# Windowed attention with soft experts: keys in blocks of 64 on stacked partitions, one exp per unit, TensorE in program order

## Chip, cores and metric

The kernel runs on one core of a Trainium2 chip. The metric is the device time of one execution in microseconds (us), the median of several runs. A profile is one execution taken by the hardware profiler; its span runs from the first to the last instruction of the program.

## The reference

Eight batches, eight heads, 576 positions of 64 numbers. Heads 0 to 3 attend to the last 32 positions, heads 4 to 7 to every fourth of the last 128. The result goes, as 4608 rows of 512, into a soft mixture of 8 experts with 4 slots each.

```python
scores = scale * np.matmul(q, k.transpose(0, 1, 3, 2))
rel = pos[:, None] - pos[None, :]
mask_plain = (rel >= 0) & (rel < 32)
mask_dil = (rel >= 0) & (rel < 32 * 4) & (rel % 4 == 0)
attn = softmax(where(mask, scores, -1e9));  x = attn @ v      # rows of 512
logits = x @ phi                                               # 4608 x 32
slot_input = softmax(logits over the rows).T @ x               # 32 x 512
slot_out[e] = relu(slot_input[e] @ w1[e]) @ w2[e]              # e of 8 experts
return softmax(logits over the slots) @ slot_out
```

Every input and the output are fp32 in HBM: q, k and v of 9.4 MB each, 33.6 MB of weights, 9.4 MB of output.

## The kernel before

**Loads.** GpSimd's queue (POOL) issues all large loads in program order (`load_batch`, L184 and L162): for each batch q, k and v, cast to fp16, into one of eight tiles `home`. The weights follow into the same tiles: `load_w1(e)` (L239) and `load_w2(e)` (L250) reuse the home of batch e once its readers are through, and stand in the main loop at the third of a batch's four units.

**Units.** A batch has four units `u` of two heads, in the order plain, dilated, plain, dilated (`unit`). A plain unit works on the 32-wide window in blocks of 128 keys (`NKB` = 5, the last one half full), each met by `QW` = 160 queries. A dilated unit sorts positions by their remainder by 4: four classes of 144, one block of 128 keys each and 16 left over, whose keys are gathered in a fifth block.

For each unit:

- `transposes(u)` (L275, L290): q and k are transposed on TensorE into the PSUM pool `ring` (2 buffers) and copied out (L280, L295) into `qT` (2 buffers) and `kTp` or `kTd`.
- `scores(u)` (L315): keys by queries into two PSUM tiles of pool `ps_s` (2 buffers of two banks). The two heads lie on the two halves of the partitions.
- `softmax_parts(u)`: exp on ScalarE, two per unit (L332 plain, L344 dilated); products with the 0/1 mask on VectorE (L335 plain, three; L353 and L360 dilated).
- `values(u)` (L395): probabilities by v (with a column of ones, which gives the sum) into two PSUM tiles of pool `ps_o` (2 buffers), all 128 keys per matmul; then reciprocal (L399) and product (L400) on VectorE, once per half.
- `x_transposes(u)` (L416): x is transposed into `ring` and copied to `xT` (L420, L422, L426).

`select_v(b)` (L205, L216, L225) rearranges a batch's v on TensorE with the 0/1 matrix `pick`, 32 rows a time, and copies it to `vp` on ScalarE; `spread_v` (L194) does the dilated heads' part on VectorE. `front_logits`, `front_rows` and `front_slots` turn a finished batch into logits, their exp `ET`, and the running sum over slots, a few units later.

**End.** After the last unit `last_early`, `last_logits` and `last_slots` finish the slots; `expert_in` (L675, L683, L686, L691) and `expert_out` (L699) run the eight experts in pairs; the sum `sop` is copied to `so` (L716); 38 matmuls `f` (L735) with copies on ScalarE and VectorE (L739, L741) make the output, which SyncE's queue stores (L745, L747).

**Order.** Only POOL keeps the order of the program (`manual_schedule`). The other engines' order is made by the scheduler of the framework from its own estimates.

## Time and profile before

| | us |
|---|---|
| median of 3 runs (185.67 to 186.18) | 185.69 |
| span of the profiled execution | 183.5 |
| TensorE matmul busy, 2595 instructions | 151.8 |
| VectorE busy, 363 | 117.1 |
| ScalarE busy, 208 | 115.5 |
| POOL busy, 77 | 46.9 |

41.06 MB, the output among them, pass the DMA queues; HBM is read for 62.02 MB and written for 9.44 MB. Some groups of instructions, with their count, the busy time of all and the mean of one:

| line, engine | what | count | us | mean ns |
|---|---|---|---|---|
| L332 ScalarE | exp, 128x960 | 16 | 15.8 | 989 |
| L332 ScalarE | exp, 128x448 | 16 | 9.1 | 572 |
| L344 ScalarE | exp, 128x640 | 32 | 20.9 | 706 |
| L335 VectorE | mask product, 128x960 | 16 | 10.3 | 646 |
| L353 VectorE | mask product, 128x1024 | 16 | 10.8 | 676 |
| L399 VectorE | reciprocal, 128x6 and 128x4 | 64 | 10.2 | 177 |
| L400 VectorE | normalising, 128x384 | 32 | 17.5 | 547 |
| L400 VectorE | normalising, 128x256 | 32 | 13.3 | 416 |
| L395 TensorE | values, 128 rows | 288 | 12.9 | 203 |
| L315 TensorE | scores, 64 rows, 160 wide | 128 | 11.1 | 256 |
| L735 TensorE | f, 512 wide | 34 | 10.6 | 417 |

Busy times of an engine's groups overlap where instructions are pipelined, so a matmul's duration is not what it costs in a row of matmuls; the distance from start to start is. In lines of the profile PE is TensorE, PEld its weight loads, DVE VectorE, ACT ScalarE, SP SyncE; a "q" behind an engine is its sequencer; behind an arrow stands what ended the idle time. PEclk in the slices is the clock that TensorE was granted, in tenths of full speed.

### The profile page before, as it was taken

What the parts mean: (1) busy time and instruction counts of PE and PEld (TensorE: products, weight loads), DVE (VectorE), ACT (ScalarE), POOL (GpSimd) and SP (SyncE); (2) the same over time, 40 slices, a digit from 0 to 9 for tenths busy, and PEclk for the clock granted to TensorE, in tenths of its full rate; (3) what the DMA queues carried; (4) which work ended last, traced back from release to release, by engine and by line L of the source; (5) the groups of instructions that cost most, each with busy time, mean ns of one, the idle gap of its engine ahead of it and who ended that gap; (6) DMA issues with size and microseconds to landing.
All of it is one profiled execution on the core that took longest, in us unless ns stands there. A gap on an engine that the chain in (4) does not pass through costs nothing.

```text
span 183.5 us, 6054 instructions
## 1 busy us (share of the span) xinstructions
PE 151.8 (83%) x2595; PEld 105.8 (58%) x2595; DVE 117.1 (64%) x363; ACT 115.5 (63%) x208; POOL 46.9 (26%) x77
## 2 busy tenths in 40 slices
PE   1869999999988989998997998898979998885300
PEld 1637776677676667666765767666768644432000
DVE  7605886388877877878779687786970111496410
ACT  2248845689599789779878959977703022675410
POOL 7752555464554654401102001003100000000000
PEclk9999999999999999999999999999995589998555
DMA  5999999999999999999999999999999995199996
GB/s 103 183 203 203 202 203 201 202 202 204 204 201 201 204 199 204 226 211 221 212 216 216 212 216 216 218 212 218 218 214 220 212 208 105 75 440 427 427 427 262
DMA packets 23978, 41.06 MB, mean 224 GB/s; under 512 B 1680, under 2 KB 20240, under 8 KB 21136
## 3 DMA queue, kind: packets, MB, share of 16 engines
q0 software_dynamic: 21584, 30.79, 93.9%
q1 hardware_dynamic: 2368, 9.89, 13.4%
q8 instruction: 20, 0.33, 0.6%
q14 instruction: 6, 0.05, 0.1%
HBM read 62.02 MB, written 9.44 MB: 389 GB/s over the span
## 4 chain that ended last, share of the span: by engine, by line
DMA 74%; issue 15%; POOL 3%; ACT 2%; DVE 1%; PE 0%; POOLq 0%; DVEq 0%; SPq 0%
DMA home<-in_moe_w_dram 31%; DMA home<-in_v_dram 15%; DMA home<-in_k_dram 12%; DMA home<-in_q_dram 9%; DMA out_dram<-ot 7%; ACT ot L739 2%; DVE ot L741 1%; POOL home L250 1%; POOL home L162 1%; POOL home L239 1%; POOL home L184 0%; POOL home L187 0%; ACT so L716 0%; PE sop L699 0%; PE f L735 0%
## 5 line engine op out<-in xcount | busy, mean ns | idle before, releaser
L400 DVE TENSOR_TENSOR x<-o,rc 128x384 f16<-128x384 f32 x64 | 29.9, 482 | 0.5
L332 ACT ACTIVATE pr<-s 128x960 f16<-128x960 f32 (+1 forms) x32 | 24.7, 780 | 1.8 <-PE s L315 1.8
L344 ACT ACTIVATE pd<-s 128x640 f16<-128x640 f32 x32 | 20.9, 706 | 1.7 <-PE s L315 1.7
L162 POOL DMA_DIRECT2D home<-in_v_dram x24 | 16.6, 692 | 16.6 <-DMA home<-in_k_dram 11.6
L205 PE MATMUL sel<-home,pick 32*128 32x256 f16 x128 | 17.8, 307 | 1.4 <-DMA home<-in_v_dram 1.1
L399 DVE RECIPROCAL rc<-o 128x6 f32<-128x6 f32 x64 | 10.2, 177 | 13.5 <-PE o L395 13.4
L416 PE MATMUL rgx<-ident,x 128*128 128x128 f16 x160 | 15.6, 233 | 3.0 <-ACT qT L295 3.0
L741 DVE TENSOR_SCALAR ot<-f,rrow 128x512 f32<-128x512 f32 (+1 forms) x19 | 12.5, 716 | 7.7 <-DMA out_dram<-ot 5.2
L335 DVE TENSOR_TENSOR Pp<-pr,mask 128x960 f16<-128x960 f16 (+2 forms) x48 | 16.4, 394 | 0.4 <-ACT pr L332 0.4
L280 ACT COPY qT<-rgq 128x576 f16<-128x576 f16 x16 | 10.3, 641 | 9.0 <-PE rgq L275 8.5
L422 ACT COPY xT<-rgx 128x512 f16<-128x512 f16 x16 | 9.6, 601 | 10.0 <-PE rgx L416 10.0
L739 ACT ACTIVATE ot<-f,rrow 128x512 f32<-128x512 f32 (+1 forms) x19 | 11.2, 675 | 7.0 <-DMA out_dram<-ot 6.6
L239 POOL DMA_DIRECT2D home<-in_moe_w_dram x8 | 4.3, 534 | 44.4 <-PE rgq L290 36.5
L213 ACT CAST vp<-sel 128x512 f16<-128x512 f32 x16 | 9.4, 590 | 9.2 <-PE sel L205 9.0
L416 PEld LDWEIGHTS <-x 128*128 128x128 f16 x160 | 10.2, 102 | 7.2 <-issue 5.4
L735 PE MATMUL f<-so,ET 128*128 128x512 f16 (+1 forms) x38 | 11.0, 402 | 3.9 <-ACT ot L739 3.0
L275 PEld LDWEIGHTS <-home 96*64 96x64 f16 x384 | 11.9, 123 | 3.9 <-issue 2.0
L184 POOL DMA_DIRECT2D home<-in_k_dram x16 | 10.6, 661 | 10.1 <-DMA home<-in_q_dram 8.2
L395 PE MATMUL o<-vp,Pp 128*128 128x65 f16 x288 | 12.9, 203 | 0.0
L436 PE MATMUL l<-xT,phi 128*128 128x288 f16 x64 | 10.8, 304 | 2.0 <-ACT qT L280 1.7
L295 DVE COPY kTd<-rgk 128x576 f16<-128x576 f16 x16 | 12.0, 752 | 0.6 <-PE rgk L290 0.5
L295 ACT COPY qT<-rgq 128x576 f16<-128x576 f16 x16 | 10.3, 646 | 3.1 <-PE rgq L290 2.6
(105 smaller groups left out, 292.9 us busy)
## 6 DMA issues: line engine op xcount, KB each, us to landing
home<-in_moe_w_dram POOLq DMA_DIRECT2D x15, 1024.0 KB, 30.1
out_dram<-ot SPq DMA_DIRECT2D x7, 1024.0 KB, 7.5
home<-in_k_dram POOLq DMA_DIRECT2D x16, 288.0 KB, 9.9
home<-in_q_dram POOLq DMA_DIRECT2D x15, 288.0 KB, 9.7
home<-in_v_dram POOLq DMA_DIRECT2D x16, 256.0 KB, 9.8
out_dram<-ot SPq DMA_DIRECT2D x3, 512.0 KB, 6.5
home<-in_moe_w_dram POOLq DMA_DIRECT2D x2, 512.0 KB, 27.3
home<-in_v_dram POOLq DMA_DIRECT2D x8, 64.0 KB, 8.9
```

Source lines behind the costliest of these rows:

```text
L162: nc.gpsimd.dma_start(out=dst, in_=v[b, h0 : h0 + n_h, r0 : r0 + 4 * n_p, :].rearrange("h (p r) d -> p h (r d)", r=4),)
L205: nc.tensor.matmul(sel[:, n, 0], pick[rows, r].rearrange("p i j -> p (i j)"), raw[rows, :, r, :], start=(r == 0), stop=(r == 3), tile_posi ...
L275: nc.tensor.transpose(rg[64 * h : 64 * h + 64, r, :], raw[:, 2 * hp + h, D * r : D * r + D], ident[0:NP, 0:NP],)
L295: (nc.scalar.copy if nm == "q" else nc.vector.tensor_copy)(out=dst[:, 0:S].rearrange("c (g p a) -> c g p a", g=4, a=3), in_=rg.rearrange(" ...
L332: nc.scalar.activation(out=pr, in_=st[:, :, 0:n], func=AF.Exp, scale=SCALE)
L335: nc.vector.tensor_tensor(out=Pp[:, :, b0 : b0 + nb, 0:w], in0=pr[:, :, at : at + nb * w].rearrange("p h (t c) -> p h t c", c=w), in1=mask ...
L344: nc.scalar.activation(out=pr[:, part].rearrange("p c e t -> p e c t"), in_=st[:, :, 0 : 2 * DW].rearrange("p e (c t) -> p e c t", c=2), f ...
L395: nc.tensor.matmul(to, lhs, rhs, start=(n == 0), stop=(n == len(mms) - 1), skip_group_check=True)
L400: nc.vector.tensor_tensor(out=x[:, blocks[0] : blocks[0] + nb, D * hl : D * hl + 2 * D].rearrange("p t (h d) -> p t h d", h=2), in0=ot[:, ...
L416: nc.tensor.transpose(rg[:, 128 * blk : 128 * blk + 128], x[:, blk, hl : hl + 128], ident)
L739: nc.scalar.activation(out=ot[:, j, d0:d1], in_=fp, func=AF.Copy, scale=scale)
L741: nc.vector.tensor_scalar(out=ot[:, j, d0:d1], in0=fp, scalar1=scale, scalar2=None, op0=ALU.mult)
```

## The change

Keys go in blocks of 64 instead of 128. Two blocks lie on the lower (`LOW`) and upper (`UP`) 64 partitions of one tile and each meets `QW` = 96 queries, so a plain unit's scores are 20 matmuls of 64 rows, 64 keys and 96 queries in a single tile `st`, and there is one exp and one mask product. A dilated unit has 16 such matmuls and 8 of 16 queries for the keys left over, one exp and two products. In `values` each matmul takes the 64 keys of one half; those of head 0's lower half go in turn with those of head 1's upper half, then, after a fence, the other two halves. The fence is an empty instruction on SyncE between the two groups. One reciprocal and one product normalise the whole unit.

`ps_s` and `ps_o` have one buffer of two banks each, `ring` has four of one; `qT` becomes two fixed tiles. `select_v` uses 64 rows a time, and the end of v has its own `select_ends`. TensorE keeps program order as POOL does, and the loop's order is written out anew: scores of the next unit, transposes, the front part of an earlier batch, `select`, first part of `values`, `x_transposes` of the unit before, second part of `values`. The experts' order becomes: input of pair n+1, transposes of pair n, output of pair n. Masks and constants follow the new blocks.

```diff
-QW = 160
+HB = 64
+QW = HB + WINDOW
+SLOT = 192
+TAIL = 16
+SLOT_D = 48 + QW
+LOW, UP = slice(0, HB), slice(HB, 128)
...
-    ring = ctx.enter_context(
-        tc.tile_pool(name="ring", bufs=2, space=bass.MemoryType.PSUM)
-    )
-    ps_o = tc.alloc_tile_pool(name="ps_o", bufs=2, space=bass.MemoryType.PSUM)
-    ps_s = tc.alloc_tile_pool(name="ps_s", bufs=2, space=bass.MemoryType.PSUM)
+    ring = tc.alloc_tile_pool(name="ring", bufs=4, space=bass.MemoryType.PSUM)
+    ps_o = tc.alloc_tile_pool(name="ps_o", bufs=1, space=bass.MemoryType.PSUM)
+    ps_s = tc.alloc_tile_pool(name="ps_s", bufs=1, space=bass.MemoryType.PSUM)
...
     def select_v(b):
+        sel = [ring.tile([128, 2, 4, D], FP32, name=f"sel{b}_{i}", tag="ring") for i in range(2)]
+        for n in range(2):
+            for r in range(4):
+                for i, part in enumerate((LOW, UP)):
+                    nc.tensor.matmul(sel[i][:, n], pick[part, n, r].rearrange("p i j -> p (i j)"), raw[part, :, r, :],
...
     def scores(u):
+        st = ps_s.tile([128, 2, 512], FP32, name=f"s{u}", tag="s")
+        def score(rows, g, at, k0, q0, n):
+            half = slice(HB * g, HB * g + HB)
+            nc.tensor.matmul(
+                st[rows, g, at : at + n],
+                kT[half, k0 : k0 + rows.stop - rows.start],
+                qT[half, q0 : q0 + n],
...
+        if hp < 2:
+            for blk in range(NKB):
+                for g in range(2):
+                    for s, rows in enumerate((LOW, UP)):
+                        k0 = 128 * blk + HB * s
+                        score(rows, g, QW * blk, k0, min(k0, S - HB), QW)
+            return st
+        for i in range(4):
+            for g in range(2):
+                score(LOW, g, QW * i, CL * i, CL * i, QW)
+                score(UP, g, QW * i, CL * i + HB, CL * (i + 1) - QW, QW)
+        for i in range(4):
+            for g in range(2):
+                q0 = CL * i + 128
+                c = 2 * (i // 2) + g
+                score(slice(0, 128), g, 4 * QW + TAIL * i, q0 - HB - TAIL * c, q0, TAIL)
...
     def softmax_parts(u, st):
+        n = NKB * QW if hp < 2 else 4 * (QW + TAIL)
+        nc.scalar.activation(out=pr, in_=st[:, :, 0:n], func=AF.Exp, scale=SCALE)
         if hp < 2:
+            nc.vector.tensor_tensor(
+                out=Pp[:, :, :, HB : HB + QW].rearrange("p h t x -> p (h t) x"),
+                in0=pr.rearrange("p h (t x) -> p (h t) x", x=QW),
+                in1=mask_p[:, None, :].broadcast_to([128, 2 * NKB, QW]),
+                op=ALU.mult,
+            )
             return
...
     def values(u):
+        ot = ps_o.tile([128, 2, 512], FP32, name=f"o{u}", tag="o")
...
+        def rest():
+            first = pairs((0, up[0]), (1, low[1]))[0]
+            tc.add_manual_dep(first, fence.name, after, reason="the other row tile is through")
+            run(tails)
+            normalise(u, ot, x, hl)
+
+        before = pairs((0, low[0]), (1, up[1]))[1]
+        fence = nc.sync.nop(nofuse=True).ins
+        tc.add_manual_dep(fence, before.name, after, reason="this row tile is through")
+        later[u] = rest
...
+    def select(u):
+        b = u // 4 + 1
+        if b < B and u % 4 == 0:
+            spread_v(b)
+            select_v(b)
+        elif b < B and u % 4 == 2:
+            select_ends(b)
...
-    ctx.enter_context(tc.manual_schedule(engines={mybir.EngineType.Pool}))
+    ctx.enter_context(
+        tc.manual_schedule(engines={mybir.EngineType.Pool, mybir.EngineType.PE})
+    )
...
     for u in range(NU + 5):
         if u + 1 < NU:
+            softmax_parts(u + 1, scores(u + 1))
+        if 0 < u and u + 3 < NU:
             transposes(u + 3)
...
+        front(u)
+        select(u)
+        if u < NU:
+            values(u)
...
         if 0 <= u - 1 < NU:
             x_transposes(u - 1)
+        if u < NU:
+            later[u]()
...
+    expert_in(0)
     for pr in range(4):
-        expert_in(pr)
-        if pr >= 1:
-            expert_out(2 * pr - 2)
-            expert_out(2 * pr - 1)
+        if pr < 3:
+            expert_in(pr + 1)
+        expert_turn(pr)
+        if pr < 3:
+            expert_out(2 * pr)
+            expert_out(2 * pr + 1)
     expert_out(6)
     expert_out(7)
```

## The prediction

> **What bounds the kernel now.** I read the page first: the slices, the queues, the chain of waits.

> ```profile
> span 183.5 us, 6054 instructions
> ...
> PEclk9999999999999999999999999999995589998555
> DMA  5999999999999999999999999999999995199996
> ...
> q0 software_dynamic: 21584, 30.79, 93.9%
> ...
> q8 instruction: 20, 0.33, 0.6%
> ```

> The DMA engines are full from the second slice (4.6 us) to about 151 us with loads, and from 160 us with stores; only two slices lie between. Then the chain of waits in order of time, around that gap (start, length, what):

> ```profile
> 128.48 28.27 DMA home<-in_moe_w_dram
> 156.74 0.04 issue
> 156.78 0.42 PE sop L699 x4
> 157.21 0.02 issue
> 157.23 0.59 ACT so L716
> ```

> The last weights land at 156.74, four matmuls consume them, `so` is copied, and the stores run to the end. Is that landing late because of the computation? By source line, a weight transfer sent from L239 lands 14.2 us after its issue at the least, and one such transfer, 1.05 MB at the 216 GB/s of the windows, takes 4.9 us: at least 9.3 us of other transfers stood ahead of it. The 3 us windows keep 210 to 227 GB/s from 75 to 144 us, so the queue never ran dry. The load stream is a floor that no faster loop lowers. The timeline shows how near the computation is to it:

> ```profile
> 155.47 1.72 PE L699 MATMUL sop<-home,hTp 128*32 128x512 f16 x23
> ...
> 156.79 0.10 PEld L699 LDWEIGHTS <-hTp 128*32 128x32 f16 x3 [0.44 <-issue]
> ```

> TensorE idled 0.44 us before the last group. Computation and loads end together: a shorter computation gains nothing, one over 0.4 us longer is paid. Last the windows, for the clock: five engines' busy times (TensorE's first), then granted clock, DMA share, GB/s.

> ```profile
> 135.00:138.00 3.00, 2.47 (x18) 2.29 (x18) 1.73 (x6) 0.00 (x0) 0.00 (x0) 1.00 1.05 221
> 138.00:141.00 3.00, 3.00 (x61) 2.65 (x59) 0.23 (x1) 0.59 (x1) 0.00 (x0) 0.50 1.02 213
> ...
> 150.00:153.00 3.00, 2.69 (x44) 1.35 (x46) 0.33 (x3) 0.60 (x1) 0.00 (x0) 1.00 0.93 187
> 153.00:156.00 3.00, 2.68 (x47) 1.36 (x43) 0.44 (x4) 0.60 (x1) 0.00 (x0) 1.00 0.39 79
> ...
> 165.00:168.00 3.00, 1.55 (x5) 0.56 (x5) 1.68 (x4) 1.40 (x3) 0.00 (x0) 1.00 1.04 437
> 168.00:171.00 3.00, 1.79 (x4) 0.57 (x4) 1.93 (x3) 1.78 (x4) 0.00 (x0) 0.62 1.02 431
> ```

> Where TensorE had little to do (135 to 138; 165 to 168, five matmuls) the clock is halved in the next window. Before the stores it is full, because the experts' matmuls fill TensorE from 145 to 157 us.

> **The change, part by part.** A unit now takes 3.75 us: by the timeline the values matmuls (L395) begin at 17.46 us and the last unit's at 133.69, 31 units on.

> Exp (ScalarE): a plain unit has 0.989 + 0.572 us (L332) and gets one of 960 elements, 0.989. A dilated one has 2 x 0.706 (L344, 640 elements) and gets one of 896; between 640 and 960 the slope is 0.283/320 us, so 0.932. Saved on average 0.53 us.

> Mask product (VectorE): plain 0.646 + 0.319 + 0.219 (L335) becomes one of 960, 0.646. Dilated 0.676 + 0.282 (L353, L360) becomes 768 elements (slope of L335's rows: 0.548) and 128 (0.219). Saved on average 0.36.

> Normalising (VectorE): 0.192 + 0.161 + 0.547 + 0.416 (L399, L400) becomes a reciprocal of 10 (slope 0.0155 each: 0.254) and a product of 640 (slope 1.02 ns: 0.809). Saved 0.25.

> TensorE: scores go from 10 matmuls to 20 (plain) and from 16 to 24 (dilated); values from 18 to 26 and from 24 to 32: 544 more in 32 units. Each has 64 rows, and quarters of the array are in no row of before; halves are (L315's two heads). Bounds: if every matmul costs its own issue, as L395's 18 in 0.72 us do ((0.72 - 0.20)/17 = 31 ns), eight to ten more are +0.3 us a unit. If the pairs run side by side, a plain unit's values are 13 x 31 ns, 0.16 us less, its scores less still: -0.3. I take 0, since L315 shows halves side by side (16 matmuls in 0.51 us) but no quarters.

> Program order on TensorE: behind a waiting matmul everything of TensorE waits, and so do ACT and DVE. New waits are single buffers: values(u) needs normalise(u-1), 1.06 us, behind scores (0.3 to 0.6) and two transposes (0.45 each): covered, up to 0.3 if not. The fence through SyncE is two hops of some 0.05 us (TensorE to ACT 0.03, ACT to TensorE 0.05 around `so`) plus a matmul's tail of 0.2, and the five L416 between, 0.45 us, cover it. Nothing else is queued on SyncE until 158.9 us; POOL's issues move nowhere, since each has the 9.3 us of queue for cover.

> At the start the order costs: select_v(1) now precedes values(0) and needs batch 1's v. POOL's timeline has batch 1's k landed at 18.8 us; the 0.26 MB behind it, at 202 GB/s, makes some 19.4 (an estimate); with its own 0.9 us (half of L205's 1.8 per batch, by pairs) values(0) begins at 20.3 instead of 17.46. If VectorE's spread_v(1), too, sits ahead of normalise(0), it waits for that batch's last v, some 4 us more.

> So a unit: 3.75 less what ACT and DVE lose (0.53, 0.61), TensorE between -0.3 and +0.3, stalls up to 0.3: bounds 3.1 and 4.0, I take 3.4, nearer the low end since every engine but TensorE loses work. Computation ends 31 x 0.35 - 2.8 = 8 us earlier, hence ahead of the loads by as much. **Worth: nothing.** Break-even, with the 0.4 us of slack, is 3.75 - 2.4/31 = 3.67 us a unit.

> Experts: the same matmuls in another order, waiting for weights that land at the old times; hidden by the stream.

> Instructions: 20 packets go with 2595 matmuls, 130 each; 3111 matmuls (+544, pp +4, select -32) make 24. One packet is 0.6% x 16 x 183.5 / 20 = 0.88 us on one DMA engine. Four over 16 engines: **+0.2 us** on the load stream; bounds -2.7 (below) and +3.5, all on the last engine.

> Clock at the tail: with the computation 8 us ahead, TensorE does in the last 5 us before 156.74 only the last two experts' output, 16 matmuls. That is the case of 165 to 168, so the final stage starts at half clock. Its price: the last sop group, 0.25 more (L675's 128x512 has 0.385 at full and 0.628 at half). A 512-wide f matmul takes 0.377, at half 0.634 (L735), issued every 0.427 (a group of four L675: 25 in 3.17 us) against 0.216 at full (five in 1.24 us at 163.69). ScalarE and VectorE (0.70 and 0.74, alternating) take one each 0.36, so TensorE becomes the limit while the store queue fills. Tile by tile: `so` +0.25, first store +0.45 (both 256-wide halves), third store (6 f) +0.9, fourth (10 f) +1.2. From there each 1.05 MB store takes 2.45 us, more than four f at half clock (1.7). Bounds 0 and 1.2; I take **+1.1**.

> Sum for the profiled execution: 183.5 + 0.2 + 1.1 = 184.8. The median, 185.69, is 2.2 above that span; the same step gives **187.0**.

> **The rivals.** *Ahead, but no price*: the clock stays full or the queue fills anyway. For it: the two expert groups may count as busy enough; against: 165 to 168 had five matmuls and halved. 185.69 + 0.2 = 185.9.
> [...]

> *TensorE becomes the bound*: loop, program order. For it: 544 more matmuls, each wait now stops all; against: ACT and DVE lose 14 to 18% of a unit. It decides from 3.67 us a unit. At 3.8: 31 x 0.13 = 4 us later, with the clock full: 189.7; at 3.9: 192.8.
> [...]
> [...]

> *The load stream evens out* (not slower): its end is that of the slowest DMA engine. For it: from 151.5 us the rate falls step by step; the 0.48 MB that the half-microsecond windows still show would at 213 GB/s end 2.7 us earlier. Instruction packets of 0.88 us are fetched at other moments now and may fall on engines with slack. Against: there are more of them. It decides if the stream ends over 1.9 us earlier; at 2.4 less and +1.1 for the clock: 184.4.

> That the change does nothing of what it says can't be: fewer exps and products are in the text.

> **How the numbers follow.** Forecast (ahead, half clock) 0.48, its own range 186.2 to 188.2; no price 0.16; TensorE the bound 0.18; evened out 0.18. Faster by over 0.3% (about what a measurement can tell here: 0.56 us) is the last, 0.18; within, the second, 0.16; slower, the rest, 0.66. The range leaves out half of each outer case: 184.6 to 190.2.

> **What would show it.** L332 and L344's successors x32 at 0.93 to 0.99; last values before 126 us; the last load near 157 and TensorE waiting for it by microseconds, not 0.44; clock 0.5 from 157 to 161; f at 0.634. Wrong: values ending after 135 (rival two), or the last load before 155 (rival three). Most of all the prediction hangs on the clock and on a load end that stays.

## The result, and the profile after

The median of four runs is 211.7 us (209.1 to 212.9), against 185.7 (185.4 to 186.2) of the kernel before beside it. Some runs of a kernel are a few per cent slower than its others (225.2 to 240.9 us in the run with small matmuls, the widest spread), so the ratios and the measured times below are those of the faster runs: here 210.1 us, ratio 1.1305 [1.1224, 1.1386], slower by 24 us. The profiled run of the kernel after is the one of 212.9 us. Its page, with span, slices and queues:

```profile
span 211.1 us, 6999 instructions
...
PEclk9995579759698558759955785695895557999955
DMA  6999999999999999999999999940299800069997
...
q0 software_dynamic: 21584, 30.79, 82.3%
...
q8 instruction: 24, 0.39, 0.7%
```

The clock now falls to half seven times between 39 and 149 us, where it stayed full in the kernel before up to 138. (The page of the kernel before shows full clock in its first slices too, but its trace records the clock only from 39.0 us on. Up to there its 128x128 transposes, L416, take some 314 ns, and 219 after; the same matmuls of the kernel after, L447, take 314 and 219 where the record says half and full. So the kernel before, too, began at half.) The loads, which ran without a break, have a hole in slices 27 to 29 (137 to 153 us) and end at 169.9 us: the queue ran dry, because the homes of the last weights came free late (POOL waits up to 18.0 us for the transposes, L291, that read them). The 24 packets are as forecast.

The chain of waits of the kernel after, in order of time (start, length, what):

```profile
159.47 0.40 PE o L405 x8
...
172.10 3.54 PE h L734 x25
...
183.28 1.08 PE sop L761 x16
184.37 0.59 ACT so L781
...
194.14 8.48 DMA out_dram<-ot
```

No load stands in this stretch. The last unit's values begin at 159.5 instead of 133.7 and run into the experts without a wait for weights; `so` is copied at 184.4 instead of 157.2, and from there to the end it is 26.7 us, as before (26.3). Nearly all of the loss arises in the start and the loop. By each unit's last reciprocal, the first unit is normalised at 29.4 us (18.9 before) and the last at 161.2 (135.1): 10.5 us lost before the first unit is through, 15.6 in the loop and 1.5 behind it.

ScalarE and VectorE did what was forecast. Groups of instructions of the kernel after (count, then busy us and mean ns, then idle time before them):

```profile
L340 ACT ACTIVATE pr<-s 128x960 f16<-128x960 f32 (+1 forms) x32 | 30.3, 946 | 33.8 <-PE s L308 33.5
L431 DVE TENSOR_TENSOR x<-o,rc 128x640 f16<-128x640 f32 x32 | 26.3, 822 | 0.6
...
L430 DVE RECIPROCAL rc<-o 128x10 f32<-128x10 f32 x32 | 7.0, 219 | 28.2 <-PE o L405 28.0
```

Exp fell from 45.8 to 30.3 us, normalising from 41.0 to 33.3, 0.48 and 0.24 us a unit. But both engines now sit idle, ScalarE 33.5 us for scores, VectorE 28.0 for values: TensorE is the bound.

What held TensorE, by its waits in the kernel after (total us, times, longest):

```profile
PE s L308 <- DVE kTd L296: 9.8, 1, 9.8
PE e L510 <- DVE Er L508: 9.5, 7, 1.5
```

The first is the start: unit 1's scores wait for `kTd`, whose copy stands on VectorE behind the copy of `spread_v(1)`, and that waits for batch 1's v until 22.8 us. The second is once a batch: in `front_rows` four matmuls with the constant `quarter` (L510) write into the tile `e` from which VectorE is still copying `Er`, and so wait for that copy of the matmuls just ahead of them. In program order everything of TensorE waits behind them. What such a wait sets off is seen in windows of the kernel after (TensorE's busy time first, then its weight loads, VectorE, ScalarE, POOL; granted clock, DMA share, GB/s). They are cut so that the wait, 49.93 to 51.38, lies in the second:

```profile
44.57:47.99 3.42, 3.42 (x67) 2.45 (x57) 1.48 (x3) 3.01 (x7) 1.80 (x3) 0.71 1.23 199
47.99:51.40 3.41, 1.96 (x74) 1.72 (x73) 3.26 (x7) 1.45 (x2) 1.49 (x3) 1.00 1.35 205
51.40:54.81 3.41, 3.41 (x79) 2.54 (x80) 1.34 (x4) 1.78 (x3) 1.94 (x4) 0.79 1.27 201
54.81:58.23 3.42, 3.42 (x92) 2.37 (x89) 2.56 (x7) 1.70 (x4) 1.25 (x2) 0.71 1.33 202
58.23:61.64 3.41, 3.41 (x101) 2.81 (x98) 2.62 (x7) 3.27 (x6) 2.15 (x4) 1.00 1.37 200
```

At full clock TensorE works 1.96 of the window's 3.41 us; behind it the clock is at half from 53.4 to 56.8 although TensorE is busy without a break. The waits that end at 87.3, 104.9, 124.2 and 142.8 us each end within 1 us of where a stretch of 6.8 to 13.7 us at half begins; at 67.0 half clock began together with the wait, so that one has another cause.

### The profile page after: what moved, and what is told of

It is laid out like the page before. It is cut to its first block, busy times and chain, and to the rows that moved or that the text cites. A ratio compares the mean times of both kernels' runs of the same rounds, so it can differ in the third digit from the quotient of the medians.

```text
span 211.1 us, 6999 instructions
## 1 busy us (share of the span) xinstructions
PE 161.1 (76%) x3111; PEld 113.2 (54%) x3111; DVE 111.3 (53%) x280; ACT 101.0 (48%) x176; POOL 47.0 (22%) x77
## 3 DMA queue, kind: packets, MB, share of 16 engines
q0 software_dynamic: 21584, 30.79, 82.3%
## 4 chain that ended last, share of the span: by engine, by line
PE 60%; DMA 14%; DVE 12%; issue 5%; ACT 3%; POOL 2%; DVEq 0%; ACTq 0%; SPq 0%; POOLq 0%
PE o L405 13%; PE rgx L447 8%; DMA out_dram<-ot 6%; PE s L308 6%; PE sel L214 5%; DMA home<-in_v_dram 5%; PE l L471 5%; DMA home<-in_k_dram 4%; DVE x L431 3%; PE rgq L276 3%; PE end L229 3%; PE h L734 3%; DVE kTd L296 2%; PE rgq L291 2%; PE rgk L276 2%
## 5 line engine op out<-in xcount | busy, mean ns | idle before, releaser
L340 ACT ACTIVATE pr<-s 128x960 f16<-128x960 f32 (+1 forms) x32 | 30.3, 946 | 33.8 <-PE s L308 33.5
L431 DVE TENSOR_TENSOR x<-o,rc 128x640 f16<-128x640 f32 x32 | 26.3, 822 | 0.6
L405 PE MATMUL o<-vp,Pp 64*128 64x65 f16 x416 | 23.4, 219 | 0.2
L430 DVE RECIPROCAL rc<-o 128x10 f32<-128x10 f32 x32 | 7.0, 219 | 28.2 <-PE o L405 28.0
L171 POOL DMA_DIRECT2D home<-in_v_dram x24 | 16.8, 700 | 16.8 <-DMA home<-in_k_dram 10.0
L405 PEld LDWEIGHTS <-Pp 64*128 64x128 f16 x416 | 16.4, 112 | 6.8 <-issue 4.5
L447 PE MATMUL rgx<-ident,x 128*128 128x128 f16 x160 | 18.5, 262 | 0.0
L308 PE MATMUL s<-qTd,kTd 64*64 64x96 f16 (+1 forms) x384 | 9.6, 208 | 9.8 <-DVE kTd L296 9.8
L806 DVE TENSOR_SCALAR ot<-f,rrow 128x512 f32<-128x512 f32 (+1 forms) x19 | 12.5, 717 | 7.6 <-DMA out_dram<-ot 5.5
L405 PE MATMUL o<-vd,Pd 64*128 64x65 f16 (+1 forms) x384 | 14.2, 207 | 1.3 <-DVE x L431 1.3
L453 ACT COPY xT<-rgx 128x512 f16<-128x512 f16 x16 | 9.4, 589 | 11.6 <-PE rgx L447 11.4
L804 ACT ACTIVATE ot<-f,rrow 128x512 f32<-128x512 f32 (+1 forms) x19 | 11.3, 672 | 7.1 <-DMA out_dram<-ot 6.6
L405 PEld LDWEIGHTS <-Pd 64*128 64x128 f16 (+1 forms) x384 | 8.9, 101 | 10.1 <-DVE Pp L342 3.6
L276 PEld LDWEIGHTS <-home 96*64 96x64 f16 x384 | 12.8, 141 | 1.6 <-DVE pick L597 0.2
L308 PEld LDWEIGHTS <-kTd 64*64 64x64 f16 (+1 forms) x384 | 6.9, 110 | 12.1 <-DVE kTd L296 9.9
L214 PE MATMUL sel<-home,pick 64*128 64x256 f16 x128 | 13.2, 374 | 0.0
L281 ACT COPY qTp<-rgq 128x576 f16<-128x576 f16 x16 | 10.2, 638 | 6.1 <-PE rgq L276 6.1
## 6 DMA issues: line engine op xcount, KB each, us to landing
home<-in_moe_w_dram POOLq DMA_DIRECT2D x2, 512.0 KB, 16.4
```

Source lines behind the costliest of these rows:

```text
L171: nc.gpsimd.dma_start(out=dst, in_=v[b, h0 : h0 + n_h, r0 : r0 + 4 * n_p, :].rearrange("h (p r) d -> p h (r d)", r=4),)
L214: nc.tensor.matmul(sel[i][:, n], pick[part, n, r].rearrange("p i j -> p (i j)"), raw[part, :, r, :], start=(n == 0 and r == 0), stop=True, ...
L276: nc.tensor.transpose(rg[64 * h : 64 * h + 64, r, :], raw[:, 2 * hp + h, D * r : D * r + D], ident[0:NP, 0:NP],)
L308: nc.tensor.matmul(st[rows, g, at : at + n], kT[half, k0 : k0 + rows.stop - rows.start], qT[half, q0 : q0 + n], start=True, stop=True, ski ...
L340: nc.scalar.activation(out=pr, in_=st[:, :, 0:n], func=AF.Exp, scale=SCALE)
L405: nc.tensor.matmul(to, lhs, rhs, start=(h not in begun), stop=True, skip_group_check=True)
```

## The experiments

All but one were timed beside the kernel before (185.7 to 185.8 us). The expectations weigh waits that program order puts in TensorE's way against TensorE's own time with more and smaller matmuls, and later against the supply of its instructions.

**Rows first.** The copy of `Er` no longer stands between the matmuls: those with `quarter` come first, the copy behind them.

```diff
             rows(ep, ..., ident[:, 0:N_SLOTS], True, True)
-            nc.vector.tensor_copy(out=Er[b % 2], in_=ep[:, 0:10])
...
+        if b < B - 1:
+            nc.vector.tensor_copy(out=Er[b % 2], in_=ep[:, 0:10])
```

> The changed kernel with one order undone: the four quarter matmuls of front_rows come before the copy of Er, so TensorE no longer waits there for VectorE (7 waits, 9.5 us in all, in the trace of after). Theory A (the wait also halves the clock: each window with it is followed by 7 to 14 us at 0.5): mean granted clock over 0.9, loop back near 3.75 us a unit, about 194.5 us, of which the late start is 8.8. Theory B (matmuls of half and quarter arrays do not count as busy, the clock falls whatever the waits): clock stays about 0.75, only the 9.5 us go, about 201 us.

Measured 202.7 us (1.088 [1.079, 1.096]), 7.4 less; the loop of the profiled run has clock 0.83. Theory A, a full clock and 194.5 us, failed; the time is near theory B's 201, though the clock rose. The wait is gone, but 17 us remain, and TensorE now idles for another reason. Its timeline in this run, after a gap that ends at 109.81:

```profile
109.81 1.65 PE L214 MATMUL sel<-home,pick 64*128 64x256 f16 x13 [2.49 <-issue]
111.06 0.83 PE L405 MATMUL o<-vp,Pp 64*128 64x65 f16 x13
```

"issue" means that nothing in the profile held it. Such gaps, 0.7 to 2.5 us, come ten times in this run, 13.6 us in all, ahead of any kind of matmul, but always a multiple of 256 instructions of TensorE (matmuls and weight loads) apart. A packet of queue q8 is 16.4 KB; 20 packets went with 2595 matmuls and as many loads, 24 with 3111, so one holds some 256 instructions. **The instructions arrive too late.** Up to 140 us each packet's transfer in this trace starts 2.9 to 4.4 us after TensorE passed the edge of one of these blocks, and the edge after is passed 2.2 us after that start at the earliest: some 6 us for 256 instructions. The kernel before has 576 a batch, 13.5 us at that rate and under its 15.0; the kernel after 712, 16.7 us (the trace has some 700, and this run's loop takes 16.1 a batch). A loop whose load stream asks for 15.0 can't be served.

**Late select.** `spread_v(1)` and the selection of batch 1 are moved in the program behind unit 3.

```diff
-        select(u)
+        if u:
+            select(u)
...
+        if u == 3:
+            select(0)
```

> The changed kernel with batch 1's spread_v and select_v moved from unit 0 to the end of unit 3; the rest as it is. If the start costs what the trace shows (scores of unit 1 wait 9.8 us for a VectorE copy queued behind spread_v(1), which waits for batch 1's v): first values matmul near 17 to 19 us instead of 26.2, and 202 to 204 us in all. If the loop is held by something else the late start is made up for: no change, 210 us.

Measured 210.1 us (1.130 [1.123, 1.137]): no gain. VectorE's order is the scheduler's, and it still put the copy of `spread_v(1)` ahead of `kTd` (wait 9.0 us), so the run doesn't say what the start costs.

**Scheduler's order.** TensorE's order is again left to the scheduler.

```diff
-    tc.manual_schedule(engines={mybir.EngineType.Pool, mybir.EngineType.PE})
+    tc.manual_schedule(engines={mybir.EngineType.Pool})
```

> The changed kernel with TensorE's order left to the scheduler again: blocks of 64, one exp and one product stay, only program order goes. Theory A (waits in program order and the clock that falls with them): clock over 0.9 and 186 to 189 us. Theory B (64-row matmuls do not keep the clock up): clock 0.75 to 0.85, over 195 us.

Measured 198.0 us (1.065 [1.055, 1.074]), clock 0.82 in the loop: program order costs 12 us of the 24. The other 12 stay with the same number of instructions. In the profiled run, 13.9 us behind that of the kernel before, 6.8 lie before the first unit is normalised (25.7 against 18.9 us), 8.0 in the loop (124.2 against 116.2), and TensorE idles at the edges of blocks, 0.4 to 2.2 us each, 11.3 in all. Theory A's 186 to 189 us failed.

**Filled wait.** Six matmuls of 512 columns, whose result is not used, stand in the wait for `Er`.

```diff
+            for _ in range(6):
+                nc.tensor.matmul(fill, ident, ones..., start=True, stop=True)
```

> The changed kernel with six 512-wide matmuls on constants added right before the waiting quarter matmuls, their result unread: the wait for VectorE stays as long, TensorE is only kept busy in it. Theory A: the clock stays full for most of the loop (over 0.88) and the time falls by 5 to 9 us, to 202 to 206 us, although work is added. Theory B, or a loop held by VectorE: no fall, 210 to 213 us.

Measured 206.1 us (1.107 [1.101, 1.114]): 4.0 us faster with work added. In the loop of the profiled runs the clock is 0.93 instead of 0.76. So part of what the wait costs is the half clock behind it; and with the clock nearly full the kernel is still 20 us behind. The loops of this run and of rows first, from the first unit's reciprocal to the last's (columns as above):

```profile
29.80:155.30 125.50, 108.60 (x2616) 77.68 (x2613) 79.70 (x183) 75.50 (x134) 28.88 (x47) 0.93 1.08 198
29.80:154.70 124.90, 109.66 (x2591) 81.49 (x2583) 79.42 (x182) 76.68 (x134) 28.68 (x47) 0.83 1.09 201
```

They are as long as each other, and TensorE idles 13.8 and 13.6 us at edges. The added matmuls take up part of what the fuller clock saves, so the equal length proves little; but the gaps at the edges stay with a nearly full clock, and so do not come from the half clock.

**Weights held.** Rows first, and the weights' loads wait until unit 28, so that the DMA queues are empty in the second half of the loop.

```diff
+    tc.add_manual_dep(held.ins, mark[28].name, after, reason="held back")
```

> The kernel of e1 (quarter matmuls first) with all weight loads held back until unit 28, so that the DMA queues are empty from about 77 us on while the loop runs; its whole time is longer, since the weights' 78 us then follow. Theory C (TensorE's instructions come in packets of 256, and while the load queue is full a packet's period can't be shorter than about 6 us; a batch of 712 instructions then takes 16.7): with empty queues the distance from packet boundary to boundary falls under 5 us, the loop between 80 and 120 us to 13 or 14 us a batch, and TensorE's waits for nothing that the profile shows are gone there. Theory B (64-row matmuls let the clock fall): the loop stays at 16.5 us a batch and the clock near 0.8.

Measured 240.8 us, since the weights follow late; the loop is what counts. Windows of this run, columns as above:

```profile
70.00:80.00 10.00, 10.00 (x177) 7.13 (x175) 5.93 (x14) 4.67 (x7) 0.00 (x0) 0.50 0.69 109
85.00:95.00 10.00, 10.00 (x315) 7.90 (x304) 8.61 (x22) 7.92 (x15) 0.00 (x0) 1.00 0.01 3
95.00:105.00 10.00, 10.00 (x281) 7.60 (x276) 8.47 (x20) 8.18 (x16) 0.00 (x0) 1.00 0.01 4
105.00:115.00 10.00, 10.00 (x284) 7.67 (x278) 8.12 (x20) 8.64 (x18) 0.00 (x0) 1.00 0.02 5
```

The clock is full for 58 us on end (82 to 140), in most of which the DMA moves 3 to 5 GB/s, and a batch takes 12.4 us, less than the 15.0 of the kernel before. All that TensorE waits for in these 58 us, none of it at an edge:

```profile
PE o L407 <- DVE x L434: 1.6, 3, 0.9
```

While the queues are empty blocks of 256 take 3.7 to 5.2 us, and a packet starts within 0.8 us of the edge. So matmuls of 64 rows in alternating shapes are not slow by themselves, and with loads in the queues the packets come later, 2.9 to 4.4 us after the edge in rows first; that they wait there behind the loads is the likely reading, but no row shows it.

**Held, but with the wait for Er.** The same hold in the kernel after, a single run.

```diff
+    tc.add_manual_dep(held.ins, mark[28].name, after, reason="held back")
```

> The changed kernel as it is, wait for Er included, with the weight loads held back until unit 28 as in x1_weights_held (loop with empty queues from about 77 us; the whole is longer for that). If the 1.45 us wait by itself halves the clock: granted clock 0.5 for parts of each batch between 85 and 125 us and 15 us or more a batch. If it took both the wait and the packets: clock 1.0 there and 14.2 us a batch (12.8 of x1 and the wait).

Measured 259.2 us; in the loop, with empty queues and no gap at an edge, `Er` waits are 16.7, 18.0 and 16.5 us apart, and the clock, over 8 us each, is 0.85 to 1.00 and 0.51 to 0.63 in turn. So the wait with its half clock alone holds a batch at 17 us, and the supply alone (rows first) at 16 to 17. Each hides the other, as far as this single run tells: only without both is the loop fast. In the kernel after itself the edges cost 3.3 us of idle time in the loop and the waits for `Er` 9.5.

**Start mended.** Rows first, the late select, and a dependence that holds the copy of `spread_v(1)` on VectorE behind unit 1's first values.

```diff
+        if b == 1:
+            tc.add_manual_dep(c.ins, mark[1].name, after, reason="not before unit 1")
```

> The kernel of e1 with batch 1's spread_v and select_v moved behind unit 1 and VectorE's copy made to follow TensorE's first values of unit 1, so that it no longer stands ahead of the copy of kTd (the scheduler had kept it there in e2). If the late start is paid in full: first values near 18 us, 7 to 8 us less than e1, 195 to 196 us. If the packets hold the loop anyway from the start: 1 to 3 us less.

Measured 198.2 us (1.067 [1.061, 1.073]), 4.5 less than rows first, between the two forecasts. The first unit is normalised at 22.1 us instead of 29.8. The last weights land at 156.8, as in the kernel before, and `so` is copied 12.0 us behind that instead of 0.5.

**Fewer instructions.** The start mended; plain values leave out six matmuls (a block's upper keys for the next block's queries), dilated ones eight of their tail, and one 384-wide matmul a unit is added: 384 instructions fewer in all.

```diff
-                for t in (3, 0, 1, 2):
+                for t in (3,):
...
-            for last in range(2):
+            for last in range(1, 2):
...
+        nc.tensor.matmul(ot[:, 0, 0:384], ident, ones..., ...)
```

> The kernel of x3 (198.15 us) with fewer instructions and the same array time: it leaves out six overflow matmuls of a plain unit's values (the neighbouring block's share) and eight of a dilated unit's tails, and adds one 384-wide matmul a unit, overwritten, which takes as long (0.16 us). 384 instructions less in all. Theory C: 48 a batch less, at 6.0 us for 256 that is 1.1 us a batch, 9 us in all: 189 us. If TensorE's array time, waits or the clock hold the loop: 197 to 199 us.

Measured 193.5 us (1.041 [1.034, 1.048]): 4.6 less, half of what was expected from the supply. Was it the instructions, or the wide matmul?

**Mended and wide.** That wide matmul alone, with nothing left out.

```diff
+        nc.tensor.matmul(ot[:, 0, 0:384], ident, ones..., ...)
```

> The kernel with rows first and the start mended (198.2, clock 0.819), and one 384-wide matmul a unit, the one that the run with fewer instructions (193.5) had too; nothing left out. Supply of instructions: 32 more matmuls are 64 more instructions, a quarter of a packet or 1.5 us; the loop stays at 16.6 us a batch or rises to 16.8, the clock rises, the time is 197 to 200, so that the 4.6 us of the other run came from its fewer instructions. Array work alone: the clock rises to 0.83 or more and the time falls to 193 to 195, so that the 4.6 us came from the wide matmul.

Measured 205.7 us (1.106 [1.098, 1.113]), 7.5 *more*, outside both forecasts. The wide matmul is no help. Between this run and the last, which differ by 224 matmuls and their 224 weight loads, lie 12.2 us; at 6 us for 256 these 448 instructions are worth 10.5. In the loops of the traces the idle time at edges is 11.4 us with the start mended, 6.7 with fewer instructions, 10.9 here; TensorE's busy time is 112.1, 109.1 and 119.2. So what fewer instructions gained lies for the most part at the edges, and what the wide matmul costs is TensorE's own time, which the idle time at the edges did not take in. Besides, the first unit is normalised 1.9 us later. So supply is not the loop's only limit.

**Small matmuls, wide matmuls, both.** The kernel before with 17 one-column matmuls a unit; with three of 384 columns; with both.

```diff
+            for _ in range(9 - half):
+                nc.tensor.matmul(ot[0:32, 0, 0, 0:1], ones[:, 0:32], ones[:, 0:1], ...)
```

```diff
+            for _ in range(2 - half):
+                nc.tensor.matmul(ot...[:, 0:384], ident, ones..., ...)
```

> The kernel before with 17 tiny matmuls more a unit (1 column, 32 rows out, overwritten by the real ones): 34 instructions, as many as the change adds, and by L475's and L457's start to start distances about 0.5 us of TensorE. Theory C: 712 instructions a batch, 16.7 us a batch instead of 15.0, about 199 us, with idle times of TensorE that end on nothing at every 256th instruction. If it is TensorE's time alone: the same as x2b_before_wide.

> The kernel before with 3 matmuls more a unit of 384 columns (overwritten by the real ones): 6 instructions and 0.49 us of TensorE, as much time as in x2a_before_tiny. Theory C: no packet limit, the loop has room for most of it, 186 to 189 us. If TensorE's time is what counts, like x2a_before_tiny.

> The kernel before with 17 one-column matmuls AND three 384-wide matmuls a unit, together what the two earlier runs added singly (230.7 with the small ones, 189.7 with the wide ones). Theory 'array work' (the traces so far: in windows of 3.41 us, rows x weight columns x columns sent, over 128 x 128, reaches 2880 in nearly all windows ahead of one at full clock, and stays under it ahead of one at half clock): the small ones alone did 2600 a window and halved the clock; 1152 more a unit lift it to about 3900, so the clock is above 0.9 and the kernel is faster than with the small ones alone although it does more: 195 to 206. Rival 'small matmuls cost this much by themselves': at least the 4 us of the wide ones on top, 234 or more, clock 0.68 as before.

Measured 226.3 us (1.218 [1.208, 1.228]), 188.1 (1.012 [1.006, 1.019]) and 208.1 (1.120 [1.113, 1.128]). As a test of the supply the first fails: it is far from the forecast 199, and TensorE never idles at an edge. But the clock is at half most of the time, with TensorE busy throughout. Windows of the run with small matmuls (profiled at 233.9 us), and of the one with both (at 218.6):

```profile
60.00:85.00 25.00, 24.79 (x421) 17.93 (x421) 13.95 (x42) 14.52 (x26) 9.27 (x16) 0.64 1.21 210
```

```profile
20.00:45.00 25.00, 25.00 (x350) 17.40 (x349) 13.49 (x39) 12.50 (x20) 12.81 (x20) 0.50 1.32 202
60.00:85.00 25.00, 23.79 (x491) 18.21 (x484) 15.57 (x46) 17.18 (x32) 8.53 (x15) 1.00 1.21 210
```

With small matmuls TensorE is busy 24.79 of 25 us at clock 0.64. With wide ones added it does more (491 matmuls instead of 421) at clock 1.00, a batch takes 18.6 us instead of 22, and the kernel is 18 us faster. So in these two runs the clock went with how much the matmuls did, not with whether TensorE was busy. The rival, 234 or more, is out. The forecast of 195 to 206 was missed by 2 us. The profiled run, slower than that, stayed at half from 11.5 to 52.4 us (first row); that half clock itself keeps the work low there is argued, not tried.

**Matmuls cut in two.** The kernel before with scores, select, logits and slots cut in two along their columns: the same array work, some 714 instructions a batch by the trace. Then with the three wide matmuls as well.

```diff
-                    nc.tensor.matmul(st[:, g, at : at + n], kT..., qT[..., q0 : q0 + n], ...)
+                    for i0, i1 in ((0, n // 2), (n // 2, n)) if n > 16 else ((0, n),):
+                        nc.tensor.matmul(st[:, g, at + i0 : at + i1], kT..., qT[..., q0 + i0 : q0 + i1], ...)
```

> The kernel before with matmuls cut in two along their columns (scores, select_v, logits, slots): the same columns and results, 1100 instructions of TensorE more, as many in all as the changed kernel has. Theory C: packets of 256 at 6.0 us, 16.7 us a batch instead of 15.0 and about 199 us, with idle times of TensorE that end on nothing at packet boundaries. If not: 186 to 188 us.

> The kernel before with its matmuls cut in two along the columns (206.9, clock 0.795), and three 384-wide matmuls a unit added. Array work: 3013 a window on average without them, many windows under 2880; with them about 4100, clock above 0.9. What is left is then the supply of instructions, 5 packets of 256 in two batches at 6 us, 15.0 us a batch and more where the work bunches: 188 to 196. If the supply binds most of the time also at full clock: 198 to 205, with idle times of TensorE at every 256th instruction. Rival 'more matmuls, more time': 210 or more.

Measured 206.9 us (1.110 [1.103, 1.117]), clock 0.79 in the loop, and 197.2 (1.062 [1.056, 1.067]), clock 0.96. Alone, cutting costs 21 us, outside both forecasts and mostly by the clock: there is one gap at an edge, 0.3 us. With wide ones added it is 9.7 us faster, between two of the forecasts, with the clock nearly full. What is left goes in part with the supply: packets start at 23.7, 29.7, 35.7, 41.8, 48.1, 54.3, 60.1, 66.0 and 72.0 us, each 5.8 to 6.3 behind the last, and TensorE idles up to 1.2 us at edges, 4.6 in all. The rest of the 11 us, with TensorE busy 118.0 instead of 107.7 us in the loop, was not separated.

**Computation ahead.** The kernel before without `select_v` from batch 2 on; later units take batch 0's and 1's v. Nothing of the change is in it: it makes the computation early, to try the load floor and the price of the clock.

```diff
-            select_v(u // 4 + 1)
+            if u // 4 + 1 < 2:
+                select_v(u // 4 + 1)
```

> The kernel before without select_v from batch 2 on (their values use batch 0's and 1's), so that TensorE and ScalarE have less to do and the computation runs ahead of the loads. The forecast's own claim: the last load lands near 157 us all the same, the clock is half when the stores begin, and the time is 186.6 to 187 us; without the price of the clock 185.7. If the loads do follow the computation: 180 us or less.

Measured 185.8 us in twelve runs (185.4 to 186.5), ratio 1.0007 [0.9989, 1.0026]. A unit takes 3.2 us, the last is normalised at 121.9 instead of 134.3, and the time stays. Its chain and windows:

```profile
121.84 34.53 DMA home<-in_moe_w_dram
156.38 0.04 issue
156.42 0.64 PE sop L700 x4
```

```profile
153.00:156.00 3.00, 0.62 (x4) 0.11 (x4) 0.00 (x0) 0.00 (x0) 0.00 (x0) 0.50 0.35 70
156.00:159.00 3.00, 1.90 (x10) 0.95 (x10) 0.60 (x2) 1.46 (x3) 0.00 (x0) 0.50 0.00 0
159.00:162.00 3.00, 3.00 (x9) 1.04 (x8) 2.45 (x4) 2.35 (x5) 0.00 (x0) 0.50 0.71 280
```

The last weights land at 156.4, as before (156.7), with 12 us more of lead. The load stream is a floor at 185.7, and a change that only shortens the computation, as this one did, doesn't beat the kernel before.

## Why the prediction was wrong

**Right:** the load stream as a floor (computation ahead: 12 us earlier, no gain); exp and normalising (0.53 and 0.25 us a unit forecast, 0.48 and 0.24 measured; VectorE's 0.61 of 3.75 us is 16%, not the 18 that the forecast gave); the 24 packets; that quarters run side by side (in the weights-held run scores matmuls start in fours within 0.01 us of each other, 20 in 0.41 us, and a batch of 12.4 us is 3.1 us a unit, the low end of the forecast's 3.1 to 4.0). Without what follows, a loop at that pace would have been ahead of the loads' 15.0, as forecast.

**Wrong, first step:** "Instructions: 20 packets go with 2595 matmuls, 130 each", then "+0.2 us on the load stream". The packets were counted rightly and priced as a load on the DMA only, not as TensorE's supply. At some 6 us a packet while the loads run, 2.78 packets make 16.7 us a batch, 4.2 a unit, and rows first measured 16.1 and 4.0: over the break-even of 3.67 that the forecast itself gave, and at the upper bound of 4.0. The count was there: 256 instructions a packet, and 2.25 packets in 15.0 us, one each 6.7. The least time of a packet was not: in the loop of the kernel before blocks take 6.4 to 7.4 us and no edge shows a gap, so the limit was near but not to be seen.

**Wrong, second step:** "Program order on TensorE", where stalls were put at "up to 0.3" and covered. The list of new waits left out `front_rows`, whose matmuls with `quarter` follow directly on the matmuls that `Er` is copied from: 1.45 us a batch, mostly with 7 to 14 us at half clock behind it. Rows first took 7.4 us off. With both steps the unit is 4.30 us ((159.5 - 26.2) / 31) where 3.4 was forecast.

**Undersized: the start.** "20.3 instead of 17.46", with 4 us more if VectorE's `spread_v(1)` came first. It did, but the victim was `kTd`, not normalising, and the first values began at 26.2. Mending it was worth 4.5 us, with rows first.

**The clock.** "+1.1" for a half-clock final stage. The run with the computation ahead has the half clock from 156 to 162 us, and from the landing to the end of the span 27.8 us instead of 26.8; its median moves by at most 0.5 (the interval's upper end). The half clock is there, its price about half or less. In the kernel after it doesn't arise: the clock is full from 176.3 to 200.2 us, where the 64 matmuls `sop` of the experts wait 1.1 us in all, so the final stage starts at full clock.

**The rival** "TensorE becomes the bound" had the side and a chance of 0.18. Its "each wait now stops all" is what rows first showed; its sign, values ending after 135 us, came (161); but the supply is not in it, and its 3.8 to 3.9 us a unit, 189.7 to 192.8 us, fell short. No run shows the 0.4 us a unit that lies between the forecast's 3.4 and this 3.8: the weights-held run changes array shapes as often as the kernel after and takes 12.4 us a batch, 3.1 a unit.

**How the 24 us add up.** Rows first 7.4, the start 4.5: 12.5 remain. In the profiled runs of the start mended and of the kernel before, 12.0 us apart, 3.2 lie before the first unit is normalised (22.1 against 18.9) and 8.6 in the loop (124.8 against 116.2). In that loop TensorE stands idle at edges for 11.4 us, where the kernel before never does; its other waits fall from 8.1 us to 1.1, and its busy time rises from 107.7 to 112.1. So the supply is the largest term of what remains. That it is the cause is borne out by the empty queues, where the gaps vanish, by the filled wait, where they stay though the clock is nearly full, and by the run with fewer instructions, where they shrink. What the half clock adds (0.81 in this loop) was not separated from it, and the 3.2 us at the start stay open. The first two terms hold in this order of mending only, since the causes hide each other.

## What to carry to other kernels

Count TensorE's instructions per stage as a resource of its own: here 256 came in no less than some 6 us while loads filled the DMA engines, so halving the height of matmuls and raising their number (2595 to 3111) cost more than what ScalarE and VectorE saved. Where an engine is put in program order, look for every matmul that waits for a copy of the one just ahead of it. And ask first what sets the end: before this change it was the loads, and nothing in the loop could gain.

## What the hardware did that was not expected

**Half clock lasted.** In the profiled run with small and wide matmuls it lasted 41 us at the start and did not come back in the 119 us after. TensorE did 350 matmuls in 25 us at half clock (20 to 45 us) and 491 at full (60 to 85), so less work per window; that this is why it lasts is likely, but no run shows it.
